# Leaving out sixteen steps of zero products on PE in the opening of a fused attention and gated-MLP kernel

## The chip, the cores and the metric

The kernel runs on one core of one Trainium2 chip. The metric is the device time of one execution in microseconds (us), the median over several executions. Engines are called as in the profile: PE (TensorE), DVE (VectorE), ACT (ScalarE), POOL (GpSimd) and SP (SyncE, whose queue issues the DMAs).

## The reference

Linear attention for 8 batches, 8 heads, 576 tokens and 64 features a head, normalised by the root of its mean square, and then a gated MLP with a product over tokens:

```
kv  = einsum('bhsd,bhse->bhde', k, v)
out = einsum('bhsd,bhde->bhse', q, kv)
x   = out / sqrt(mean(out*out, -1) + 1e-6) * g_norm      # then heads side by side: (8, 576, 512)
h   = gelu(x @ w_in)                                     # tanh form, 512 -> 1024
u, v = h[..., :512], h[..., 512:]
v_n = (v - mean(v)) / sqrt(var(v) + 1e-6) * g_ln
v_s = einsum('ts,bsd->btd', w_sg, v_n) + b_sg[None, :, None]
y   = x + (u * v_s) @ w_out
```

## The kernel before, in words

Every large product is made of three products of float32r halves (high by high, high by low, low by high), so weights and activations are split into a rounded part and a rest: ACT makes the rounded part, DVE or POOL the rest. w_in and w_out come as 64-bit words and are turned into float32 by a chain of integer steps for each of 16 pieces: A (ACT), B, E and L (DVE; L is `word_sign`, line 245), C (POOL, `word_add`, line 248), F (ACT, `weight_high`, line 259) and I (`weight_low`, DVE or POOL, lines 277 to 284). D loads a piece; D16 to D19 load the four blocks of w_sg into two buffers ("stage", line 208), so D18 and D19 can only be issued when the rests of the first two blocks (line 280) are made.

What each engine does, and in which order, is written out by hand in one table, `ORDER`. A name in it is a letter for the step, then the batch, then an index. The steps that matter here, with the tile names that the profile shows:

- k, q: loads of k and v (line 296) and of q (334), issued on SP. SP's queue is in order.
- K (`kv`, line 305, tile pkv): k times v for one block of tokens; c (`kv_high`, line 325) copies the finished matrix out of PSUM on ACT. Batch 0 has K00 to K04, batch 1 K10 to K14.
- o (line 353, tile po): q times that matrix, eight products a batch. f (`o_scale`, line 365 on ACT, 367 on DVE) copies one out with the factor g_norm, e (`o_square`, line 357, ACT, tile sq) squares it, s (`sums`, line 375, tile pss) adds the squares on PE.
- t, j (`rstd`, `newton`, lines 391 to 407): the inverse root by integer estimate and Newton steps, on DVE. For batch 0, T (line 436, y_parts, DVE) and M (line 442, tile pb, PE) spread it over the partitions and x (line 447, DVE) multiplies. From batch 1 on it goes over DRAM (r, lines 413 to 418, tile bc) and x is line 450.
- X, Y (lines 454 and 458): rounded part and rest of x. U (line 540, tile pu) and V (489, pv) are the first products with w_in; P, S and the others follow.
- N (`warm`, line 185, tile warm): two products of a 128x128 block of zeros with 512 columns of zeros. Their PSUM tile is read by nobody.

```
    def warm(*_):
        ps = PS("warm")
        for _ in range(2):
            nc.tensor.matmul(ps, kvh[:, 0, :], kvh.rearrange("p a b -> p (a b)"), start=True, stop=True)
```

The table holds 44 N steps, N00 to N43, all of them ahead of U00, the first product with w_in: 18 from the start to the middle of the run ahead of o00, six more behind them in the same run, and the rest scattered in ones, twos, a three (N33 to N35) and a seven (N37 to N43) between the steps of batch 1 and the first K of batch 2. PE's queue is in order too, so an N step is done before the product behind it, whether that product is ready or not.

Of the kernel before, what the change touches and what calls it, by code (L numbers as in the profile page):

```python
# [10 lines left out]
U32 = mybir.dt.uint32  # L11
# [27 lines left out]

ORDER = """  # L40
    k00 k01 k02 k03 N00 k04 N01 K00 D22 N02 D00 K01 D01 N03 N04 D02 K02 N05 D03 N06 N07 q00 K03 N08 D21 N09 N10 q01
    K04 q02 F22 N11 c00 N12 c01 N13 q03 A00 N14 N15 E00 N16 B00 q10 A01 N17 L00 N18 E01 C00 N19 q11 B01 N20 N21 N22
    D24 F00 N23 L01 k10 I00p o00 F21 o01 k11 f00v e00 o02 e01 f01v C01 o03 A02 f02v k12 s00 e02 B02 o04 F01 E02 o05
    f03a f04v I01p o06 k13 e03 f05v e04 L02 o07 e05 s01 f06a f07v C02 s02 A03 k14 N24 e06 E03 N25 F02 B03 K10 D04
    e07 I02p L03 N26 D05 K11 D06 s03 N27 t00 k20 C03 K12 t01 N28 N29 q12 F03 t02 t03 K13 q13 I03v N30 t04 D16 K14
    t05 N31 j00 c10 j01 N32 c11 D17 j02 A04 o10 j03 j04 o11 e10 B04 k21 N33 A05 E04 N34 j05 e11 N35 B05 f10a T00 s10
    E05 f11a o12 D07 T01 T02 o13 D23 f12a T03 M04 T04 M06 e12 M02 f13v D20 M07 e13 o14 x07v o15 L05 e14 M01 F16 s11
    f14v C05 x01v e15 o16 f15v F17 M00 I16p s12 x06v f16a K20 x00v e16 I17v X00 o17 D18 M05 Y00p x02v M03 D19 f17a
    D08 x05v e17 N36 D09 x03v F20 s13 k22 x04v N37 t10 N38 k23 L04 X01 I21p N39 t11 N40 X02 N41 F18 N42 C04 N43 Y01v
    F19 m0 t12 F04 I19v F05 t13 q20 X03 I05v K21 t14 A06 Y02v Y03p t15 U00 k24 I18v k30 j10 h20 E06 q21 j11 I04v U02  # L50
    u00 j12 n00 A07 j13 n01 j14 U03 E07 u02 j15 B07 r10 n02 L07 K22 u03 n03 U06 C07 h21 k31 B06 c20 c21 r11 F07 U07
    d21 L06 u06 I07v C06 U01 u07 d20 A08 I20v F06 K30 l10 u01 r12 l11 l12 U04 l13 I06v m1 k32 E08 B08 A09 k33 V00
    n10 u04 L08 E09 C08 B09 F08 D10 n11 n12 L09 V01 n13 C09 I08v F09 D11 x10p x11v a00 I09p V02 b00 r13 a01 i20v p00
    i21v q22 y00 q23 K31 b01 z00 o20 k34 w00 p01 o21 e20 V03 k40 e21 a02 y01 b02 x13p z01 h22 w01 U05 p02 i22v a03
    x12p y02 q30 V04 u05 X10 X11 Y10v X12 Y11p b03 z02 K32 Y12v a04 k41 p03 X13 w02 Y13p V10 b04 A10 y03 p04 E10 z03
    V11 B10 L10 y04 C10 w03 z04 D12 F10 w04 S00 A11 I10v E11 S01 a10 g00 b10 G00 B11 H00 p10 S02 L11 J00 C11 g01 y10
    G01 F11 D13 S03 g02 I11p H01 J01 G02 A12 S04 g03 B12 G03 H02 E12 S05 H03 J02 g04 L12 G04 J03 P00 C12 H04 g05 J04
    G05 F12 D14 P01 Q00 I12v A13 S06 E13 Q01 B13 L13 C13 S07 g06 F13 D15 G06 I13v V12 A14 g07 z10 E14 G07 B14 w10
    L14 A15 U15 C14 E15 F14 B15 V13 f20a L15 I14v u15 C15 f21a a11 F15 b11 I15p P03 p11 a12 b12 P02 y11 p12 Q03 z11
    U16 Q02 H05 w11 H06 H07 J05 o22 a13 J06 o23 e22 b13 U12 u16 h23 f22v p13 J07 f23a P06 i23p y13 u12 e23 P07 q31  # L60
# [612 lines left out]
```

## Time and profile before

| | |
|---|---|
| median of 3 runs | 529.02 us (528.95 to 529.67) |
| profiled execution, its own time | 528.13 us |
| its span, first to last instruction | 526.3 us |
| PE busy | 516.1 us, 98% of the span |
| DVE, ACT, POOL busy | 313.5, 200.4, 189.3 us |
| mean granted TensorE clock | 0.996 of full speed |

Busy times are sums over the whole span; a share near 100% says which engine the bulk waits for, and says nothing on the opening, where N steps count as busy too. Times in the rows further down are microseconds from the span's start. In a row of a timeline, the bracket at the end gives the idle time of the engine ahead of the row and who ended it.

### The profile page before, as it was taken

To read this page: it belongs to the slowest core of one execution; us is meant where nothing else is said; L and a number is where in the kernel's file an instruction comes from. 1 tells how busy PE (TensorE), PEld (TensorE's weight loads), DVE (VectorE), ACT (ScalarE), POOL (GpSimd) and SP (SyncE) were. 2 spreads that over 40 slices of the span, in tenths; PEclk is the share of its full clock that TensorE was granted. 3 is DMA by queue.
4 is the path that set the end of the run, shared out by engine and by line. 5 is a ranking of instruction groups with operands and counts; after the bars stand their busy time and mean duration, and the time that the engine had idled before them with its cause. 6 is when DMAs were issued, how large, how long until landed. Compare 5 with 4: busy or idle time off the path is not lost.

```text
span 526.3 us, 10121 instructions
## 1 busy us (share of the span) xinstructions
PE 516.1 (98%) x4032; PEld 476.2 (90%) x4032; DVE 313.5 (60%) x656; ACT 200.4 (38%) x449; POOL 189.3 (36%) x215
## 2 busy tenths in 40 slices
PE   7999899999999999999999999999999999999997
PEld 5765888999999989999999988999999989999997
DVE  0489877867376676645557556646277557841433
ACT  1358545344532336314533325423353325221210
POOL 1345267643345324521044204623117206520230
PEclk9999899999999999999999999999999999999999
DMA  8987684111363455001363144002121221002002
GB/s 249 371 277 263 209 225 152 42 42 52 108 209 94 169 158 149 24 1 45 109 205 102 68 143 100 22 24 68 47 74 45 91 57 40 2 1 91 0 24 69
DMA packets 33723, 55.51 MB, mean 105 GB/s; under 512 B 7308, under 2 KB 9228, under 8 KB 33676
## 3 DMA queue, kind: packets, MB, share of 16 engines
q1 hardware_dynamic: 33676, 54.86, 33.3%
q8 instruction: 32, 0.52, 0.4%
q14 instruction: 15, 0.12, 0.1%
HBM read 44.90 MB, written 9.95 MB: 104 GB/s over the span
## 4 chain that ended last, share of the span: by engine, by line
PE 95%; DMA 2%; POOL 1%; ACT 1%; DVE 0%; SPq 0%; issue 0%; POOLq 0%
PE pu L540 20%; PE pg L554 19%; PE py L586 19%; PE pv L489 18%; PE po L353 5%; PE pkv L305 4%; PE warm L185 4%; PE pg L557 3%; PE pss L375 2%; DMA kv_first<-in_vx 1%; DMA v<-in_vx 1%; POOL xo L458 1%; DVE x L367 0%; SPq L296 0%; ACT sq L357 0%
## 5 line engine op out<-in xcount | busy, mean ns | idle before, releaser
L586 PE MATMUL py<-g,woh 128*128 128x288 f32 x512 | 106.6, 296 | 0.0
L567 POOL TENSOR_TENSOR gt<-gt,u 128x288 f32<-128x288 f32 x64 | 56.4, 887 | 88.4 <-DVE gt L562 79.7
L586 PEld LDWEIGHTS py<-g,woh 128*128 128x128 f32 x512 | 83.7, 188 | 0.3
L554 PE MATMUL pg<-wsh,vh 128*128 128x288 f32 x256 | 75.8, 296 | 0.0
L554 PE MATMUL pg<-wso,vh 128*128 128x288 f32 x256 | 75.6, 295 | 0.0
L586 PE MATMUL py<-g,woo 128*128 128x288 f32 x256 | 75.5, 295 | 0.0
L554 PE MATMUL pg<-wsh,vo 128*128 128x288 f32 x256 | 75.5, 295 | 0.0
L504 POOL TENSOR_SCALAR rs<-mv 128x1 f32<-128x1 f32 x36 | 12.3, 343 | 126.0 <-DVE mv L500 125.3
L574 ACT CAST g<-gt 128x288 fp32r<-128x288 f32 x64 | 27.1, 432 | 79.8 <-POOL gt L567 77.5
L562 DVE SCALAR_TENSOR_TENSOR gt<-pg,glt,b_bc 128x288 f32<-128x288 f32 x64 | 32.8, 515 | 38.2 <-PE pg L557 37.7
L591 DVE SCALAR_TENSOR_TENSOR x<-py,x 128x288 f32<-128x288 f32 x64 | 29.2, 457 | 43.9 <-PE py L586 43.1
L545 ACT ACTIVATE u<-pu 128x288 f32<-128x288 f32 x64 | 26.3, 411 | 62.8 <-PE pu L540 62.3
L586 PEld LDWEIGHTS py<-g,woo 128*128 128x128 f32 x256 | 48.2, 188 | 0.2
L554 PEld LDWEIGHTS pg<-wsh,vh 128*128 128x128 f32 x256 | 48.1, 188 | 0.3
L554 PEld LDWEIGHTS pg<-wso,vh 128*128 128x128 f32 x256 | 48.1, 188 | 0.1
L554 PEld LDWEIGHTS pg<-wsh,vo 128*128 128x128 f32 x256 | 48.2, 188 | 0.0
L540 PE MATMUL pu<-xh,wuh 128*128 128x288 f32 x256 | 45.9, 301 | 0.0
L540 PE MATMUL pu<-xh,wuo 128*128 128x288 f32 x256 | 44.3, 295 | 0.0
L540 PE MATMUL pu<-xo,wuh 128*128 128x288 f32 x256 | 44.3, 295 | 0.0
L499 DVE BATCH_NORM_STATS2 st<-hv 128x6 f32<-128x512 f32 x32 | 22.2, 693 | 33.6 <-ACT hv L494 33.4
L578 DVE TENSOR_TENSOR g<-gt,g 128x288 fp32r<-128x288 f32 x64 | 36.7, 588 | 9.0 <-ACT g L574 9.0
L540 PEld LDWEIGHTS pu<-xh,wuh 128*128 128x128 f32 x256 | 38.1, 190 | 1.6 <-issue 0.5
(108 smaller groups left out, 1025.8 us busy)
## 6 DMA issues: line engine op xcount, KB each, us to landing
q<-in_qT SPq DMA_DIRECT2D x32, 288.0 KB, 4.0
out_y<-x SPq DMA_DIRECT2D x28, 288.0 KB, 2.1
bc<-rd SPq DMA_DIRECT2D x28, 256.0 KB, 4.0
k<-in_kx SPq DMA_DIRECT2D x24, 256.0 KB, 4.4
v<-in_vx SPq DMA_DIRECT2D x24, 256.0 KB, 4.5
kv_first<-in_kx SPq DMA_DIRECT2D x8, 256.0 KB, 5.7
kv_first<-in_vx SPq DMA_DIRECT2D x8, 256.0 KB, 6.1
words<-in_wu SPq DMA_DIRECT2D x4, 512.0 KB, 7.7
```

The source lines that it names most:

```text
L353: nc.tensor.matmul(ps[:, :HS], a, m[:, t], start=(i == 0), stop=(i == len(terms) - 1))
L489: nc.tensor.matmul(pv, a[cc], w[:, cc, :], start=(n == 0), stop=(n == 11))
L499: ve.bn_stats(st, hv_[b, c])
L540: nc.tensor.matmul(pu[:, :HS], w[:, cc, f], a[b, cc][:, t], start=(i == 0), stop=(i == 11))
L545: ac.activation(u_[b, n], part["u", b, n][:, :HS], AF.Gelu_apprx_tanh, scale=W_UP)
L554: nc.tensor.matmul(ps[:, :HS], a[:, d], w[:, c, t], start=(i == 0), stop=False)
L562: ve.scalar_tensor_tensor(g_[b, n], ps[:, :HS], glt[:, dc : dc + 1], b_bc[:, half(n // 4)], op0=ALU.mult, op1=ALU.add)
L567: po.tensor_tensor(g_[b, n], g_[b, n], u_[b, n], op=ALU.mult)
L574: ac.copy(gs_[b, n][0], g_[b, n])
L578: ve.tensor_tensor(lo, g_[b, n], f32(hi), op=ALU.subtract)
L586: nc.tensor.matmul(ps[:, :HS], w[:, dc, block(n % 4)], a, start=(i == 0), stop=(i == 11))
L591: ve.scalar_tensor_tensor(xs, y_[b, n][:, :HS], W_UP, xs, op0=ALU.mult, op1=ALU.add)
```

## The change

Sixteen N steps are taken out of `ORDER`: N18 to N23 ahead of o00, N24 to N32 between the steps of batch 1, and N36 ahead of the last sum of batch 1. The other 28 stay, and all other steps keep their places. One line of the table as an example:

```
-    K04 q02 F22 N11 c00 N12 c01 N13 q03 A00 N14 N15 E00 N16 B00 q10 A01 N17 L00 N18 E01 C00 N19 q11 B01 N20 N21 N22
-    D24 F00 N23 L01 k10 I00p o00 F21 o01 k11 f00v e00 o02 e01 f01v C01 o03 A02 f02v k12 s00 e02 B02 o04 F01 E02 o05
+    K04 q02 F22 N11 c00 N12 c01 N13 q03 A00 N14 N15 E00 N16 B00 q10 A01 N17 L00 E01 C00 q11 B01 D24 F00 L01 k10 I00p
+    o00 F21 o01 k11 f00v e00 o02 e01 f01v C01 o03 A02 f02v k12 s00 e02 B02 o04 F01 E02 o05 f03a f04v I01p o06 k13
```

The table is a line shorter, so each line number below it falls by one in the changed kernel. On PE, from the last K of batch 0 to the last K of batch 1 (pkv is K, warm is N, po is o, pss is s), there stood:

```order
L305 MATMUL pkv<-v,k 64x64 x8
L185 MATMUL warm<-kvh 128x512 x26
L353 MATMUL po<-q,kvf 128x288 x4
L375 MATMUL pss<-sq,ones 32x144 x4
L353 MATMUL po<-q,kvf 128x288 x4
L375 MATMUL pss<-sq,ones 32x144 x8
L185 MATMUL warm<-kvh 128x512 x4
L305 MATMUL pkv<-kv_first 64x64 x8
L185 MATMUL warm<-kvh 128x512 x2
L305 MATMUL pkv<-kv_first 64x64 x8
L375 MATMUL pss<-sq,ones 32x144 x4
L185 MATMUL warm<-kvh 128x512 x2
```

and the same stretch, with what follows up to the three N steps that are left, is now:

```order
L304 MATMUL pkv<-v,k 64x64 x8
L184 MATMUL warm<-kvh 128x512 x14
L352 MATMUL po<-q,kvf 128x288 x4
L374 MATMUL pss<-sq,ones 32x144 x4
L352 MATMUL po<-q,kvf 128x288 x4
L374 MATMUL pss<-sq,ones 32x144 x8
L304 MATMUL pkv<-kv_first 64x64 x16
L374 MATMUL pss<-sq,ones 32x144 x4
L304 MATMUL pkv<-kv_first 64x64 x16
L304 MATMUL pkv<-v,k 64x64 x8
L352 MATMUL po<-q,kvf 128x288 x2
L184 MATMUL warm<-kvh 128x512 x6
```

The run of 26 products ahead of the first po is now 14, and between there and the po of batch 1 no zero product is left. DVE, ACT and POOL keep every instruction in its place. SP keeps the order of its DMAs too, but the two w_sg loads D18 and D19 have changed buffers, and with them their waits. Before, on SP (stage is w_sg, words w_in or w_out; the brackets name the engines and DMA queues waited for):

```order
L211 DMA wl<-in_wsl 128x576 [waits DMAHW6_49,DVE_49]
L208 DMA stage<-in_ws 128x576 [waits DMAHW7_49,DMAHW0_49,Pool_49]
L208 DMA stage<-in_ws 128x576 [waits DMAHW1_49,DVE_49]
L205 DMA words<-in_wo 128x512
L205 DMA words<-in_wo 128x512 [waits DMAHW2_49]
L296 DMA k<-in_kx 128x512 [waits DMAHW3_49,PE_49]
L296 DMA v<-in_vx 128x512 [waits DMAHW4_49]
```

and with the change:

```order
L210 DMA wl<-in_wsl 128x576 [waits DMAHW6_49,DVE_49]
L207 DMA stage<-in_ws 128x576 [waits DMAHW7_49,DMAHW1_49,DVE_49]
L207 DMA stage<-in_ws 128x576 [waits DMAHW0_49,Pool_49]
L204 DMA words<-in_wo 128x512
L204 DMA words<-in_wo 128x512 [waits DMAHW2_49]
L295 DMA k<-in_kx 128x512 [waits DMAHW3_49,PE_49]
L295 DMA v<-in_vx 128x512 [waits DMAHW4_49]
```

The first of the two stage loads now waits for DVE and the second for POOL; it was the other way round.

## Rows read from the trace of the kernel before

**Rows 1.** The page: busy times of PE, and the chain that ended last, by engine

```profile
PE 516.1 (98%) x4032; PEld 476.2 (90%) x4032; DVE 313.5 (60%) x656; ACT 200.4 (38%) x449; POOL 189.3 (36%) x215
...
PE 95%; DMA 2%; POOL 1%; ACT 1%; DVE 0%; SPq 0%; issue 0%; POOLq 0%
```

**Rows 2.** Timeline of PE, 16 to 57 us: start, duration, instruction, idle time before

```profile
16.83 6.19 PE L185 MATMUL warm<-kvh 128*128 128x512 f32 x26
22.86 2.10 PE L353 MATMUL po<-q,kvf 128*128 128x288 f32 x8
...
35.90 0.68 PE L305 MATMUL pkv<-v,k 64*64 64x64 f32 x16
...
55.52 1.12 PE L305 MATMUL pkv<-v,k 128*64 128x64 f32 x16 [0.18 <-DMA v<-in_vx]
56.57 1.26 PE L540 MATMUL pu<-xh,wuh 128*128 128x288 f32 x4
```

**Rows 3.** Timeline of DVE, 20 to 46 us

```profile
22.15 0.14 DVE L269 TENSOR_SCALAR g<-gnt 128x1 f32<-128x1 f32 x1
23.54 0.52 DVE L367 TENSOR_SCALAR x<-po,g 128x288 f32<-128x288 f32 x1 [1.25 <-PE po L353]
...
32.35 0.31 DVE L391 TENSOR_SCALAR rstd<-pss 128x144 f32<-128x144 f32 x1 [1.13 <-PE pss L375]
32.70 1.01 DVE L393 TENSOR_SCALAR rstd<-rstd 128x144 int32<-128x144 int32 x1
...
38.10 0.43 DVE L241 TENSOR_SCALAR w<-w 128x512 int32<-128x512 int32 x1 [0.50 <-ACT w L233]
...
39.64 1.49 DVE L436 SCALAR_TENSOR_TENSOR y_parts<-yh,ext,rstd 32x144 fp32r<-32x144 f32 x4
41.70 0.52 DVE L367 TENSOR_SCALAR x<-po,g 128x288 f32<-128x288 f32 x1 [0.57 <-PE po L353]
...
42.60 0.69 DVE L245 SCALAR_TENSOR_TENSOR w<-words,w 128x512 int32<-128x512 int32 x1
```

**Rows 4.** Timeline of ACT, 28 to 38 us

```profile
30.56 0.41 ACT L357 ACTIVATE sq<-po 128x288 f32<-128x288 f32 x1
33.65 0.62 ACT L259 CAST wuh<-w 128x512 fp32r<-128x512 f32 x1 [2.68 <-POOL w L248]
36.63 0.74 ACT L325 COPY kvf<-pkv 64x256 f32<-64x256 f32 x2 [2.36 <-PE pkv L305]
```

**Rows 5.** Timeline of POOL, 30 to 46 us

```profile
30.74 1.62 POOL L277 TENSOR_TENSOR wuo<-w,wuh 128x512 fp32r<-128x512 f32 x1 [0.73 <-ACT wuh L259]
32.32 1.29 POOL L248 TENSOR_TENSOR w<-w,words 128x512 int32<-128x512 int32 x1
...
44.67 1.44 POOL L280 TENSOR_TENSOR wso<-stage,wsh 128x576 fp32r<-128x576 f32 x1
```

**Rows 6.** Waits of SP's queue, 40 to 62 us: total, times, longest

```profile
SPq L208 <- POOL wso L280: 4.4, 1, 4.4
```

**Rows 7.** The load of v issued at 50.53 us (line 296): time to landing

```profile
DMA to landing us min/median/max: 4.8/4.8/4.8
```

**Rows 8.** Stretches: length, PE busy, PEld, DVE, ACT, POOL, granted clock, DMA share, GB/s

```profile
22.90:28.80 5.90, 5.44 (x42) 3.13 (x40) 4.48 (x9) 4.27 (x11) 3.09 (x4) 1.00 1.04 336
...
37.50:48.20 10.70, 10.70 (x98) 6.93 (x97) 9.47 (x23) 8.38 (x19) 4.49 (x3) 1.00 0.78 275
...
51.60:54.20 2.60, 0.01 (x1) 0.02 (x1) 2.32 (x4) 2.09 (x6) 0.80 (x1) 1.00 0.96 336
54.20:57.60 3.40, 3.20 (x36) 2.94 (x37) 3.40 (x7) 1.34 (x2) 1.41 (x1) 0.50 0.58 188
```

**Rows 9.** Timeline of POOL, 81 to 91 us

```profile
81.28 1.30 POOL L450 TENSOR_TENSOR x<-x,bc 128x512 f32<-128x512 f32 x1 [2.03 <-DMA bc<-rd]
...
84.34 1.28 POOL L450 TENSOR_TENSOR x<-x,bc 128x512 f32<-128x512 f32 x1
86.74 1.43 POOL L458 TENSOR_TENSOR xo<-x,xh 128x576 fp32r<-128x576 f32 x1 [1.12 <-ACT xh L454]
```

More of the change, by code (lines that the diff above doesn't have):

```diff
@@ L46 @@
[L46 to L60, printed above, removed]
@@ new lines @@
+    o00 F21 o01 k11 f00v e00 o02 e01 f01v C01 o03 A02 f02v k12 s00 e02 B02 o04 F01 E02 o05 f03a f04v I01p o06 k13
+    e03 f05v e04 L02 o07 e05 s01 f06a f07v C02 s02 A03 k14 e06 E03 F02 B03 K10 D04 e07 I02p L03 D05 K11 D06 s03 t00
+    k20 C03 K12 t01 q12 F03 t02 t03 K13 q13 I03v t04 D16 K14 t05 j00 c10 j01 c11 D17 j02 A04 o10 j03 j04 o11 e10 B04
+    k21 N33 A05 E04 N34 j05 e11 N35 B05 f10a T00 s10 E05 f11a o12 D07 T01 T02 o13 D23 f12a T03 M04 T04 M06 e12 M02
+    f13v D20 M07 e13 o14 x07v o15 L05 e14 M01 F16 s11 f14v C05 x01v e15 o16 f15v F17 M00 I16p s12 x06v f16a K20 x00v
@@ new lines @@
+    e16 I17v X00 o17 D18 M05 Y00p x02v M03 D19 f17a D08 x05v e17 D09 x03v F20 s13 k22 x04v N37 t10 N38 k23 L04 X01
+    I21p N39 t11 N40 X02 N41 F18 N42 C04 N43 Y01v F19 m0 t12 F04 I19v F05 t13 q20 X03 I05v K21 t14 A06 Y02v Y03p t15
+    U00 k24 I18v k30 j10 h20 E06 q21 j11 I04v U02 u00 j12 n00 A07 j13 n01 j14 U03 E07 u02 j15 B07 r10 n02 L07 K22
+    u03 n03 U06 C07 h21 k31 B06 c20 c21 r11 F07 U07 d21 L06 u06 I07v C06 U01 u07 d20 A08 I20v F06 K30 l10 u01 r12
+    l11 l12 U04 l13 I06v m1 k32 E08 B08 A09 k33 V00 n10 u04 L08 E09 C08 B09 F08 D10 n11 n12 L09 V01 n13 C09 I08v F09
@@ new lines @@
+    D11 x10p x11v a00 I09p V02 b00 r13 a01 i20v p00 i21v q22 y00 q23 K31 b01 z00 o20 k34 w00 p01 o21 e20 V03 k40 e21
+    a02 y01 b02 x13p z01 h22 w01 U05 p02 i22v a03 x12p y02 q30 V04 u05 X10 X11 Y10v X12 Y11p b03 z02 K32 Y12v a04
+    k41 p03 X13 w02 Y13p V10 b04 A10 y03 p04 E10 z03 V11 B10 L10 y04 C10 w03 z04 D12 F10 w04 S00 A11 I10v E11 S01
+    a10 g00 b10 G00 B11 H00 p10 S02 L11 J00 C11 g01 y10 G01 F11 D13 S03 g02 I11p H01 J01 G02 A12 S04 g03 B12 G03 H02
+    E12 S05 H03 J02 g04 L12 G04 J03 P00 C12 H04 g05 J04 G05 F12 D14 P01 Q00 I12v A13 S06 E13 Q01 B13 L13 C13 S07 g06
@@ new lines @@
+    F13 D15 G06 I13v V12 A14 g07 z10 E14 G07 B14 w10 L14 A15 U15 C14 E15 F14 B15 V13 f20a L15 I14v u15 C15 f21a a11
+    F15 b11 I15p P03 p11 a12 b12 P02 y11 p12 Q03 z11 U16 Q02 H05 w11 H06 H07 J05 o22 a13 J06 o23 e22 b13 U12 u16 h23
+    f22v p13 J07 f23a P06 i23p y13 u12 e23 P07 q31 Q06 y12 O06 z12 P05 Q07 z13 w12 O07 w13 P04 Q05 O05 o24 Q04 o25
+    e24 O04 U14 e25 h30 f24a i30p U13 u14 f25a q32 o26 u13 o27 f26v e26 U11 h31 c30 i31p c31 d30 U17 u11 d31 f27a
+    q33 e27 o30 u17 o31 f30v s20 h32 f31a i32p K40 t20 e30 t21 e31 o32 k42 o33 t22 e32 f32v U10 k43 h33 f33v q40 e33
@@ new lines @@
+    i33p t23 o34 u10 o35 e34 S10 q41 e35 t24 t25 j20 j21 j22 S11 g10 j23 G10 j24 h40 K41 j25 H10 i40p g11 J10 S12
+    k44 G11 k50 r20 H11 S13 g12 q42 J11 G12 S14 H12 g13 J12 G13 S15 H13 g14 r21 J13 G14 r22 P11 H14 g15 J14 G15 P12
+    Q11 l20 l21 l22 l23 S16 m2 Q12 n20 n21 n22 S17 n23 g16 x21p x20v P10 G16 g17 X20 r23 G17 X21 Y20v P13 Y21p Q10
+    K42 Q13 H15 H16 J15 k51 H17 J16 J17 P17 P16 Q17 O17 x23v x22p P15 Q16 O16 X22 P14 Q15 f34a Y22v O15 f35a X23 o36
+    Q14 o37 Y23p e36 f36v O14 V20 h41 f37v c40 i41p c41 d40 e37 d41 q43 s30 a20 b20 K50 t30 p20 U26 k52 t31 t32 y20
@@ new lines @@
+    k53 t33 z20 V21 t34 u26 w20 t35 j30 j31 j32 j33 V22 a21 j34 j35 b21 r30 p21 V23 y21 a22 z21 b22 r31 w21 p22 r32
+    K51 a23 y22 U23 b23 z22 k54 k60 w22 p23 U21 l30 u23 l31 l32 l33 y23 m3 U22 z23 n30 n31 n32 x30p u21 w23 o40 u22
+    o41 e40 x31p U25 h42 f40v e41 n33 f41a V24 r33 i42v u25 q50 o42 a24 o43 f42a K52 b24 h43 U20 k61 f43v p24 e42
+    e43 i43p y24 o44 u20 o45 e44 U24 x33p e45 q51 x32v h50 z24 U27 i50v u24 w24 S20 q52 u27 X30 X31 Y30v S21 X32 g20
+    X33 Y31v G20 S22 g21 Y32p H20 J20 S23 Y33p g22 G22 V30 g23 G21 G23 H21 H22 J21 H23 J22 S24 a30 J23 b30 p30 P21
@@ new lines @@
+    g24 G24 y30 P23 H24 Q21 J24 P20 Q23 S25 Q20 V31 g25 G25 P22 a31 b31 S26 Q22 H25 p31 J25 y31 S27 g26 G26 H26 V32
+    g27 z30 J26 G27 z31 w30 H27 J27 P27 w31 a32 b32 U35 Q27 p32 O27 y32 P26 z32 u35 w32 f44a U36 Q26 f45a O26 U32
+    u36 o46 u32 P24 f46v e46 U31 Q24 O24 P25 u31 o47 Q25 U33 h51 f47v O25 c50 i51v c51 U37 e47 d50 q53 u33 d51 o50
+    u37 o51 f50a s40 f51v h52 K60 t40 e50 i52v e51 o52 t41 q60 o53 t42 k62 f52a t43 V33 t44 f53a k63 t45 h53 j40 j41
+    e52 i53p j42 e53 o54 a33 o55 q61 j43 U34 e54 b33 h60 j44 p33 e55 j45 U30 r40 u34 i60p y33 K61 u30 z33 k64 w33
@@ new lines @@
+    r51 a41 b41 V42 r52 p41 k74 y41 z41 V43 a42 l50 l51 l52 l53 w41 m5 b42 U40 n50 p42 a43 n51 n52 n53 x50p b43 V44
+    u40 x51v p43 y42 r53 z42 y43 w42 z43 K72 a44 w43 U45 b44 U42 p44 u45 y44 z44 o60 o61 x53p U44 f60a w44 h62 x52p
+    u42 S40 u44 i62v X50 X51 S41 Y50p X52 Y51v q70 e60 e61 f61a S42 Y52p X53 g40 g41 S43 g42 Y53p G42 V50 G40 G41
+    H40 J40 H41 g43 V51 H42 J41 a50 G43 J42 H43 b50 o62 J43 a51 p50 P41 f62v e62 b51 P43 y50 p51 Q41 y51 P40 Q43 P42
+    Q40 o63 Q42 o64 f63a S44 h63 e63 i63v e64 S45 q71 g44 G44 H44 o65 g45 S46 e65 J44 G45 h70 i70p H45 S47 J45 q72
@@ new lines @@
+    X60 J53 r63 X61 Y60p H54 P51 g55 J54 Y61p P52 g56 Q51 n61 G56 n62 P53 G55 Q52 n63 S57 x63v x62p Q53 P50 X62 g57
+    G57 X63 Y62p Y63v V60 H55 H56 Q50 H57 J55 J56 J57 P55 a60 b60 P54 Q55 p60 O55 y60 P56 z60 Q54 O54 w60 f74a P57
+    Q56 f75a O56 o76 Q57 o77 e76 f76v O57 U66 f77a e77 s70 u66 U61 t70 t71 t72 t73 t74 U65 t75 u61 j70 j71 j72 U63
+    j73 u65 j74 j75 r70 V61 u63 r71 V62 a61 r72 b61 p61 V63 y61 a62 l70 z61 l71 l72 l73 w61 m7 b62 U60 a63 n70 p62
+    n71 n72 n73 x70p b63 V64 u60 y62 x71p z62 w62 U67 p63 r73 a64 b64 U62 y63 u67 p64 z63 y64 U64 u62 w63 z64 u64
@@ new lines @@
+    w64 S60 X70 x72p X71 x73v S61 X72 Y70v Y71p X73 S62 g60 g61 G60 G61 H60 S63 g62 Y72p H61 Y73v V70 G62 J60 H62
+    J61 J62 V71 g63 a70 G63 b70 H63 p70 J63 P61 y70 a71 b71 P63 Q61 p71 y71 P62 Q63 P60 Q62 S64 Q60 S65 g64 G64 H64
+    S66 g65 J64 G65 S67 H65 g66 J65 G66 U76 H66 g67 z70 J66 G67 z71 w70 U75 u76 H67 w71 J67 P65 u75 P66 Q65 O65 P67
+    Q66 O66 U77 Q67 O67 P64 u77 U72 Q64 O64 V72 u72 V73 a72 b72 p72 U70 y72 a73 z72 b73 U71 w72 u70 p73 U74 y73 u71
+    z73 w73 S70 u74 S71 g70 G70 H70 S72 g71 J70 G71 U73 H71 g72 J71 G72 S73 u73 H72 J72 S74 g73 G73 H73 S75 g74 J73
@@ L106 @@
+    G74 P71 H74 g75 J74 G75 P73 Q71 H75 O71 J75 S76 Q73 O73 S77 g76 G76 H76 P70 g77 J76 G77 P72 Q70 H77 O70 J77 P74
+    Q72 O72 P75 Q74 O74 P76 Q75 O75 P77 Q76 O76 Q77 O77
 """.split()
```

57 lines of the change are left out of this document (10 added, 47 removed).

## The prediction, made before the changed kernel had run

> **What bounds the kernel now.** I read the page first: PE is busy for 516.1 of 526.3 us, and the chain that ended last is 95% PE [rows 1]. So the bulk is PE's own work, and a change ahead of it can only matter by the moment at which that bulk starts. The timeline of PE has it at 56.57 us: the first product with w_in, behind two K steps that waited for v [rows 2]. From there on the list of PE's waits is empty, to the end. So the question is how much earlier the product at 56.57 starts, and whether what feeds PE later keeps up. In the opening PE looks busy throughout, but 18 us of that are zero products; there I read the waits of the other engines: DVE waits for PE at 23.54, 32.35 and 41.70 [rows 3], ACT at 36.63 [rows 4], and SP's queue waits 4.4 us for POOL [rows 6]. These name the path.
>
> **The change part by part.**
>
> *A zero product's price.* The 26 products ahead of o00 lie between 16.83 and 22.86 [rows 2]: 0.232 us each, 0.464 a step. Sixteen steps are 7.4 us of PE. That is the ceiling, and the path takes little of it.
>
> *Six steps ahead of o00: 1.2 us of their 2.8.* PE would reach o00 at 20.1 instead of 22.86, if its q is there (no row of mine shows the landing; even if it came at 21.5, the copy named next would not be later, since the first product takes some 0.7). What waits for o00 is the DVE copy at 23.54, after 1.25 idle. The instruction ahead of it ends at 22.29 [rows 3]. So the copy starts at about 22.3: **1.2 earlier**. The other 1.6 becomes idle time on PE.
>
> *N24 to N26 and the sum: 2.1.* Copies and squares of batch 0 follow one another on DVE and ACT and end with the square at 30.56 to 30.97 [rows 4]; being fed by that copy, it moves 1.2, to an end at 29.75. The sum behind it ends in time for DVE's 32.35 [rows 3], but was then held not by the square but by PE's queue, zero products included. Three of these steps (1.4) are gone on top of the 1.2, so PE is there 2.6 earlier and waits for the square: the sum, 0.45 long, ends at about 30.2, and DVE starts at 30.3, **2.1 earlier**.
>
> *The root on DVE: 1.5 at its end.* DVE now meets POOL's two instructions at 30.74 and 32.32 [rows 5], which have only moved by 1.2, in other places. The row at 32.70 took 1.01 us and ended just after POOL's row of 32.32; I let one DVE row wait for that POOL row again. ACT's row at 33.65 waits for the same POOL row, and DVE's 34.30 for ACT, so at this point the gain is only 1.0. A second wait, 0.50 for ACT at 38.10 [rows 3], goes: ACT stood behind the copies at 36.63, which waited 2.36 for PE [rows 4], and PE's K14 at 35.90 [rows 2] has seven more steps (3.2 us) out of its way. That makes 1.5: the four rows from 39.64 end at 39.6 instead of 41.13.
>
> *N30 to N32 and the wait at 41.70: 2.1.* DVE then idled 0.57 for PE [rows 3]. With the copies of 36.63 at about 33.3, behind ACT's 33.65 less 1.0 [rows 4], the products of 37.54 [rows 2] run near 34.2; the three N steps that stay (1.4) and four more products end near 38.3. So DVE goes on at 39.6: **2.1 earlier**, and with it the L245 at 42.60 [rows 3] and POOL's L280 of 44.67 [rows 5], which ends SP's wait of 4.4 [rows 6].
>
> *SP and the loads of batch 2: 2.1.* Behind that wait SP issues two stage loads, two words, and the k and v for which PE waits at 55.52. The swapped waits of the two stage loads price at nothing: both were issued one behind the other and both rests are needed before the second. Were the first to be late by the 0.6 between the two rests, its ACT copy stands behind other work. The last v took 4.8 us to land [rows 7], as before, so the K behind it starts at 53.4 instead of 55.52, and the products of 56.57 at about **54.5, 2.1 earlier**. N36's two products (0.46) sit ahead of a sum that waits for its square; I give them nothing, and 0.5 in the range.
>
> *The clock: 0 to 1.05 given back.* PE was idle from 51.6 to 54.2, the granted clock then stood at 0.50 (the lower level, 1.2 GHz) until 57.6, and at 1.00 (2.4 GHz) in all the stretches ahead, also where PE had short waits, 5.44 busy in 5.90 [rows 8]. Today 1.05 of dense work falls into the low stretch (56.57 to 57.6), which costs 0.5. If that stretch moves with the idle time, this is unchanged. If it stays where it is, 3.1 of dense work falls into it, costing 1.55, or 1.05 more. I take 0.4, between the two. New idle on PE is shorter than the 2.6 that was followed by the fall: about 1.3 near 22 to 23.4, 1.0 near 29, 1.7 from 32.5 to 34.2. By the rows I price these at no fall. The Trainium skill ("TensorE: Matmul & The Clock Gate", section "A second HAM failure mode: psum-queue depth-cycling") tells of a kernel whose PE idled shortly but often between groups of products, and whose clock went to and fro for it; no row here shows that, and by it the sum would be that of the first rival.
>
> *Later: the gain must pass 81 to 91 us.* The chain of waits leaves PE once more, for POOL's xo rows at 86.74 and 89.79, which PE awaits at 91.2. They begin with ACT work that PE itself feeds, but POOL's x of 81.28 waits for a DMA, and the x of 84.34 ends at 85.62 [rows 9]. If that DMA does not move, the row at 86.74 can come 1.1 earlier and no more. It should move, since its issue goes back over DVE and POOL rows to a K of batch 2 near 62, which PE reaches earlier. Bounds 1.1 and 2.1.
>
> **Sum.** 2.1 less 0.4 is 1.7 us. The profiled execution took 528.13 (526.3 of span, 1.8 around it) and would take 526.4. It lies 0.9 under the median of the three runs; against that median the forecast is 529.02 - 1.7 = **527.3 us**.
>
> **The rivals.**
>
> *Slower: the clock falls in the opening.* With its filling gone PE does 5.3 us of real products between 22.9 and 28.8, and 3 between 28.8 and 37.5. If the clock falls there, it can be low for the products with q and for K20, in the stretch 37.5 to 48.2, where PE is busy all the time and DVE and ACT wait for it by turns [rows 8]. A low stretch as long as the one seen (3.4) costs at most 1.7 where PE is waited for. One such stretch eats the gain: 529.0. Two turn it: 527.3 + 3.4 = 530.7; low from 28.8 to 48, with 8 us of real products in the last part at half speed less the waits they fill, gives some 533. It decides from two stretches on PE's path. For it: no stretch with so much short idling exists in the trace. Against it: the full clock with 5.44 busy in 5.90, and that slower products fill the gaps by themselves.
>
> *No change: lost on the way.* The path above passes from engine to engine six times. If POOL and DVE meet badly (rows like the 1.01 at 32.70 instead of a few tenths), or if the chain at 81 to 91 holds its DMA, 0.6 to 1.2 is left: 527.9 to 528.4.
>
> *More than forecast.* If the low stretch is missed altogether and SP's issues close up, PE's bulk may start up to 3.1 earlier: 525.9.
>
> **How the numbers follow.** No change can be told from one here within 0.2%, 1.06 us: 527.96 to 530.08. The forecast (525.9 to 527.9) has 0.55, the lost gain and one low stretch, both within the bound, 0.28, and two or more low stretches 0.17. So faster 0.55, same 0.28, slower 0.17. The range goes from 525.8, the largest gain, to 530.6, where about a tenth is left above; the forecast's own range is 525.9 to 527.9.
>
> **What would show it.** Right: PE's first po near 20.3; the DVE copy near 22.3; DVE's L391 (now L390) near 30.3; its y_parts ending near 39.6; SP's two stage loads near 44; PE's first pu near 54.5; a granted clock of 1.00 from 16 to 50 us; and no PE wait longer than now behind 91 us. Wrong: a clock of 0.50 anywhere from 23 to 48 us, a square or copy that keeps its old time, or a first pu that is earlier while POOL's xo at 89.79 is not.

## The result: slower by 0.8%, and the profile after

The changed kernel took 532.92 us (median of 7 runs, 531.76 to 534.45), the kernel before 529.43 in the same session (7 runs, 528.42 to 530.07): ratio 1.0077, 95% interval 1.0056 to 1.0098. Forecast were 527.3 us and a range up to 530.6; it went the other way. The profiled execution took 531.76 us with a span of 530.0, 3.7 more than the span of 526.3 before. In two of the kernels further down (the changed kernel again, and the same padded) a single run of 1262 and of 1268 us is counted in the median and left out of the ratio.

The page of the changed kernel, busy times and the chain that ended last (to set beside [rows 1]):

```profile
PE 510.1 (96%) x4000; PEld 471.5 (89%) x4000; DVE 316.1 (60%) x656; ACT 200.8 (38%) x449; POOL 189.1 (36%) x215
...
PE 89%; DMA 8%; POOL 1%; SPq 1%; ACT 1%; issue 0%; DVE 0%; DVEq 0%; POOLq 0%
```

PE has 32 products less and is busy 6.0 us less, and yet the whole is longer: what was PE's share of the chain is now DMA's, 8% where there were 2%. PE's timeline from the first product with q on (po; to set beside [rows 2]) says where:

```profile
22.04 2.18 PE L352 MATMUL po<-q,kvf 128*128 128x288 f32 x8 [1.05 <-POOL w L247]
...
29.77 0.69 PE L304 MATMUL pkv<-kv_first 128*64 128x64 f32 x16 [0.76 <-DMA kv_first<-in_vx]
...
33.26 0.69 PE L304 MATMUL pkv<-kv_first 128*64 128x64 f32 x16 [1.47 <-DMA kv_first<-in_vx]
34.83 0.68 PE L304 MATMUL pkv<-v,k 64*64 64x64 f32 x16 [0.88 <-DMA v<-in_vl]
36.45 2.07 PE L352 MATMUL po<-q,kvf 128*128 128x288 f32 x4 [0.94 <-ACT kvf L324]
37.90 2.77 PE L184 MATMUL warm<-kvh 128*128 128x512 f32 x6
...
56.13 0.69 PE L304 MATMUL pkv<-v,k 128*64 128x64 f32 x16 [3.99 <-DMA v<-in_vx]
57.45 1.12 PE L304 MATMUL pkv<-v,k 128*64 128x64 f32 x16 [0.63 <-DMA v<-in_vx]
58.50 1.33 PE L539 MATMUL pu<-xh,wuh 128*128 128x288 f32 x4
```

Four short waits stand where the zero products stood. Behind them four products with q took 2.07 us and six zero products 2.77; before it was

```profile
37.54 1.18 PE L353 MATMUL po<-q,kvf 128*128 128x288 f32 x4
38.35 1.77 PE L185 MATMUL warm<-kvh 128*128 128x512 f32 x6
```

The rows at 56.13 and 57.45 are K21, the second K of batch 2, in two parts (K20 runs near 46 us, and the seven N steps from N37 on stand between the two). The wait ahead of it grew from 2.60 to 3.99, and the first product with w_in (pu), 56.57 before, stands at 58.50. The stretches of the changed kernel (columns as in rows 8) give the clock:

```profile
28.80:37.50 8.70, 4.53 (x83) 3.43 (x80) 7.86 (x18) 3.00 (x7) 3.57 (x3) 0.95 1.06 332
36.60:40.10 3.50, 3.50 (x9) 2.55 (x10) 3.01 (x11) 2.56 (x6) 0.00 (x0) 0.51 1.05 385
...
57.10:60.50 3.40, 3.05 (x24) 2.97 (x25) 3.37 (x12) 0.67 (x1) 0.00 (x0) 0.50 0.47 128
```

and the first of them before:

```profile
28.80:37.50 8.70, 8.70 (x110) 5.82 (x107) 7.26 (x17) 2.90 (x8) 4.08 (x3) 1.00 0.82 248
```

There are two stretches at the lower level (0.50, 1.2 GHz; called low stretches from here on): the one behind the wait for K21's v, as in before [rows 8], and a new one from 36.6 to 40.1 us. PE had been busy for 4.53 of the 8.70 us from 28.8, where before it had been busy throughout. DVE's timeline (to set beside [rows 3]) shows an early gain and its loss:

```profile
23.07 0.52 DVE L366 TENSOR_SCALAR x<-po,g 128x288 f32<-128x288 f32 x1
...
31.03 0.31 DVE L390 TENSOR_SCALAR rstd<-pss 128x144 f32<-128x144 f32 x1 [0.28 <-PE pss L374]
...
38.94 1.50 DVE L435 SCALAR_TENSOR_TENSOR y_parts<-yh,ext,rstd 32x144 fp32r<-32x144 f32 x4
42.26 0.52 DVE L366 TENSOR_SCALAR x<-po,g 128x288 f32<-128x288 f32 x1 [1.82 <-PE po L352]
```

0.47 earlier at the first copy, 1.32 at the root's first row, 0.70 at y_parts. Then DVE waits 1.82 us for products that start late and run at the lower clock, and the copy that stood at 41.70 stands at 42.26, 0.56 late. From PE's po at 36.45 to this copy it is 5.81 us; before, from 37.54 to 41.70, it was 4.16, so the lower clock cost some 1.65 here. The two stage loads whose waits were swapped are issued at 47.29 instead of 46.13, but closer together, and the last v behind them at 51.09 instead of 50.53: late by the same 0.56, so the swap added nothing. The flight of that v, 6.2 us instead of 4.8, makes the rest of the 1.93 by which the first pu is late. By PE's first product with w_out (105.5 us before, 108.2 now) 2.7 of the 3.7 us of loss stand; most of the rest is one wait of 0.7 us for a DVE copy further on.

One more row does not fit a story of the clock alone. The eighth load of the program (v of K03) is issued at 4.0 us in both kernels, when nothing that differs between them has run. Time from its issue to its landing, before:

```profile
DMA to landing us min/median/max: 6.1/6.1/6.1
```

and in the changed kernel:

```profile
DMA to landing us min/median/max: 9.7/9.7/9.7
```

SP's queue passes this on. It waits for these loads before it issues the weights, and the first q, issued at 10.77 us before, is issued at 13.98. (The bracket of the po at 22.04 names POOL, but this q landed at 21.90.) The chain that ended last, followed back from PE's K14, is then a row of loads, each issued when the one before it has landed (start, duration):

```profile
13.98 7.92 DMA q<-in_qT
22.29 5.90 DMA kv_first<-in_vx
28.21 6.58 DMA v<-in_vl
34.83 0.71 PE pkv L304 x16
```

In the kernel before PE's own work, zero products included, stands in that place of the chain from 7.62 to 23.5 us and from 27.49 to 50.3 us.

### The profile page after: what moved, and what is told of

It is laid out like the page before. It is cut to its first block, busy times and chain, and to the rows that moved or that the text cites. A ratio compares the mean times of both kernels' runs of the same rounds, so it can differ in the third digit from the quotient of the medians.

```text
span 530.0 us, 10057 instructions
## 1 busy us (share of the span) xinstructions
PE 510.1 (96%) x4000; PEld 471.5 (89%) x4000; DVE 316.1 (60%) x656; ACT 200.8 (38%) x449; POOL 189.1 (36%) x215
## 4 chain that ended last, share of the span: by engine, by line
PE 89%; DMA 8%; POOL 1%; SPq 1%; ACT 1%; issue 0%; DVE 0%; DVEq 0%; POOLq 0%
PE pu L539 19%; PE pg L553 19%; PE py L585 19%; PE pv L488 18%; PE po L352 5%; PE pkv L304 3%; PE pg L556 3%; DMA kv_first<-in_vx 3%; PE pss L374 2%; DMA q<-in_qT 1%; DMA v<-in_vl 1%; DMA v<-in_vx 1%; DMA out_y<-x 1%; PE warm L184 1%; SPq L295 1%; POOL xo L457 1%
```

## The experiments

All ratios are to the kernel before, run on the same chip in the same session; the number of runs is in brackets. There were four sessions, each on another chip: the first four experiments, the next four, the next three and the last four. Kernels of different sessions are best compared by their ratios. "Behind N43" is the place behind the last fourteen zero products ahead of K21, where PE waits for v. Some of the texts on record call this step K20.

### Which half of the change, and the wait ahead of K21

**Six steps out** (N18 to N23 alone):

```diff
-A01 N17 L00 N18 E01 C00 N19 q11 B01 N20 N21 N22 D24 F00 N23 L01
+A01 N17 L00 E01 C00 q11 B01 D24 F00 L01
```

> Only the six steps ahead of the first product with q are out; the ten later ones stay. Clock theory (without its filling PE has short idle times, the granted clock falls to 0.50 between 28 and 50 us in most executions, and slow products on the path cost more than the steps): here nearly all of the filling is still there, so the clock stays at 1.00 up to 50 us and the kernel is 0 to 1.2 us faster than before (the first copy on DVE comes 1.2 earlier): 528.2 to 529.4. Load theory (the changed kernel is slow because its first loads of k and v landed some 3 us later than before, which has nothing to do with the N steps): the time follows the landings of the first loads in this run's trace, 529 if they are as before. Path theory (the sum of the prediction, which needs no clock): 1.0 to 1.2 faster.

Measured: 530.69 us (12 runs), ratio 1.0031 (1.0009 to 1.0053). Slower, against the clock and the path expectations: the clock held up to 55 us, and the eighth load took 9.4 us, as the load expectation would have it.

**Ten steps out** (N24 to N32 and N36 alone):

```diff
-k14 N24 e06 E03 N25 F02
+k14 e06 E03 F02
...
-x05v e17 N36 D09
+x05v e17 D09
```

> Only the ten later steps (N24 to N32 and N36) are out; the six ahead of the first product with q stay. Clock theory: the clock falls in the stretch 28 to 50 us as in the changed kernel, mean granted clock 0.99 or lower, 531.5 to 533.5. Load theory: as before, 529, unless its first loads are late. Path theory: 0 to 1 faster, 528.4 to 529.4.

Measured: 533.62 us (7 runs), ratio 1.0076 (1.0044 to 1.0108). The trace has a low stretch from 36.3 to 43.1 us; its eighth load took 9.4 us too.

**The changed kernel again**, with no edit:

> The changed kernel once more, for a second trace and more clocks. Clock theory: 532 to 534 again, with at least two low stretches of the clock ahead of 57 us, also when the first loads land as in the kernel before. Load theory: when the first loads land as in the kernel before (the fourth load by 7.5 us) the time is 529 or less.

Measured: 533.02 us (12 runs), ratio 1.0065 (1.0041 to 1.009). Its five runs with a mean clock of 0.983 to 0.987 took 533.6 to 535.1 us, the six with 0.990 to 0.994 530.3 to 532.5; the runs of before beside them had 0.993 to 0.999. The profiled execution, 530.67 us, has no low stretch ahead of 53 us, against the clock expectation; its eighth load was late again (8.8 us).

**A bridge** (before, with six more zero steps, N50 to N55, behind N43):

```diff
-C04 N43 Y01v
+C04 N43 N50 N51 N52 N53 N54 N55 Y01v
```

> The kernel before with six more N steps behind N43, in the 2.6 us in which PE idles for v ahead of the second K of batch 2. Clock theory: the clock no longer falls at 54.2, the K and the first products with w_in run at 1.00, and 0.5 to 1.0 us are gained: 528.4 to 528.9. If zero products don't hold the clock, or if the low stretch costs nothing: 529.4, or up to 0.3 more where the six steps (2.8 us) reach past the arrival of v.

Measured: 526.85 us (11 runs), ratio 0.9945 (0.9926 to 0.9964): more work on PE makes the kernel 2.5 us faster. PE's timeline, with the twelve products in the place of the 2.60 us of idle time:

```profile
47.94 6.23 PE L185 MATMUL warm<-kvh 128*128 128x512 f32 x26
54.10 0.69 PE L305 MATMUL pkv<-v,k 128*64 128x64 f32 x16
55.23 0.69 PE L305 MATMUL pkv<-v,k 128*64 128x64 f32 x16 [0.44 <-DMA v<-in_vx]
55.84 0.80 PE L540 MATMUL pu<-xh,wuh 128*128 128x288 f32 x4
```

K21 runs at 0.69 a part where it took 1.12, the first products with w_in take 0.80 where they took 1.26 [rows 2]. The trace has no low stretch between 13 and 520 us. So PE's idle time ahead of K21 brings the low stretch of the kernel before. Between the two traces the span differs by 1.2 us only (526.3 and 525.1), with a low stretch of 3.4 us in before; a second trace of before (below) has one of 6.8. The runs bear out the rest: of all 114 runs of before in the four sessions, the ten with a mean clock of 0.998 or more took 526.4 to 528.2 us, as with the bridge, and the 49 with 0.994 or less had a median of 530.1. So the low stretch was worth most of the 2.5 us. And each part of the change alone loses, the ten steps more than the six by their medians (the intervals overlap a little).

### The length of PE's program

The late loads were in all kernels with fewer products on PE than before has, and not in the others. The chip does not part the two: on the first one the bridge's eighth load took 6.5 us beside 8.8 to 9.4 of the three shorter programs, on the second one it is 9.0 of the one shorter program beside 5.8 to 7.4. To tell chance from cause, the next kernels get their count back by short products of 64 columns behind PE's last product, where PE has nothing left to do.

**The changed kernel, padded** with 32 of them:

```diff
+    def pad(*_):
+        ps = PS("pad")
+        for _ in range(2):
+            nc.tensor.matmul(ps[:, :64], kvh[:, 0, :], kvh[:, 0, :64], start=True, stop=True)
...
-O77
+O77 W00 W01 W02 W03 W04 W05 W06 W07 W08 W09 W10 W11 W12 W13 W14 W15
```

> The changed kernel with 32 short zero products (64 columns) behind its last product, where PE idles while the last stores land, so that PE's program has as many instructions as before. Clock theory: nothing changes, 532 to 534, mean clock 0.983 to 0.994. Program theory (the first loads land late, the eighth near 14 us instead of 10.8, in the four kernels with a shorter PE program, because the program's size shifts where things lie in memory): the eighth load lands near 11 us and 1 to 1.5 us are gained, 531 to 532.

Measured: 531.58 us (10 runs), ratio 1.0043 (1.0011 to 1.0074). The eighth load took 7.2 us, as the program theory had it; a low stretch from 34.3 to 37.8 us stays.

**Before again**, one execution:

> The kernel before, unchanged, for a second trace. Program theory: the eighth load lands near 11 us again. If the first loads merely vary between executions, it can land anywhere between 10.8 and 14. Clock theory: clock 1.00 from 13 to 50 us whatever the loads do, and one or two low stretches near 54 us.

Measured: 527.94 us. Its eighth load took 5.8 us.

**The changed kernel with the bridge:**

> The changed kernel with the six N steps behind N43. It is to part the low stretch at 54 us from those in the opening. Clock theory: the first is gone, those between 28 and 50 us stay, so it is 2 to 3 us faster than the changed kernel but 2 to 4 slower than the kernel before with the same six steps (526.85): 529 to 531. If the changed kernel's loss is all at 54 us, it comes to 527.

Measured: 532.49 us (12 runs), ratio 1.0067 (1.0041 to 1.0093). The bridge alone does not help the changed kernel, and both expectations missed. Its eighth load took 9.0 us, and the trace has low stretches from 33.6 to 40.4 and from 57.4 to 64.3 us. Its five runs with a mean clock of 0.995 to 0.999 still took 530.1 to 533.3 us, so the clock is not the whole loss.

**Six steps moved** (N18 to N23 out, the bridge in, so PE's count is that of before):

> The six steps ahead of the first product with q are moved behind N43; the other 38 stay, and the number of instructions is that of the kernel before. Clock theory: no low stretch, 526 to 527, as fast as with the six steps added, or up to 1.2 faster by the earlier first copy. Program theory: the eighth load lands near 11 us; then the 1.4 us that the kernel without the six was slower than before are explained, and it is 525.7 to 526.9. If the six steps are needed where they stand, 528 or more.

Measured: 526.23 us (12 runs), ratio 0.9935 (0.9911 to 0.9959), within the first two expectations.

**Six steps out, padded** (twelve short products at the end):

> Only N18 to N23 out, as in the run of that name without a bridge, and twelve short zero products (64 columns) behind PE's last product, which bring PE's instruction count back to that of before. Length theory: loads that were issued before anything differed came late in the kernels with a shorter PE program (the eighth load landed at 13.97 us there, at 10.76 and 10.88 in before), so with the count restored the eighth load lands by 12 us, the last v of K20 needs about 5 us instead of 7.0, the first product with pu starts a us earlier than in before and the time is 528 to 529.5. Clock theory alone: the loads are late by chance, PE waits as long ahead of the v loads, and the time stays at 530.7 with the low clock at 55 to 62 us.

Measured: 528.17 us (12 runs), ratio 0.997 (0.995 to 0.9991); without the pad it was 1.0031 (1.0009 to 1.0053). Twelve products that run after all other products make the kernel 0.0061 of its time faster, 3.2 us. The clock alone does not explain it: at the same mean clock of 0.994 the six runs without the pad took 530.3 to 533.7 us and the five with it 528.4 to 529.0, while before had medians of 529.7 and 529.8 at this clock in the two sessions. The last v still took 6.3 us, not the five expected.

**All out, bridge and pad** (twenty short products):

> The changed kernel with six zero steps behind N43 and twenty short zero products behind PE's last product, so that PE's count is that of before. Length theory: the eighth load lands by 12 us, K13 and K14 wait little, no or one low stretch in the opening, and the time is 527 to 529 (before the bridge alone: 532.5). Clock theory: the opening still has a low stretch at 34 to 43 us, since the ten later steps are missing, and the time is 529.5 to 532. If the length says nothing: 532.5 again, eighth load at 13 to 14 us.

Measured: 529.45 us (12 runs), ratio 1.0009 (0.9992 to 1.0027); without the pad 1.0067 (1.0041 to 1.0093). The eighth load landed at 12.1 us; the time lies between the two theories' ranges, and the opening has its low stretch.

**Before, padded** (twelve):

> The kernel before with twelve short zero products behind PE's last product: the price of the pad itself and a control of the length theory on the long side. Both theories: the eighth load at 10.5 to 12 us, the clock as in before, and the time 529.2 plus 0 to 1.0 for the pad.

Measured: 529.14 us (12 runs), ratio 1.0003 (0.999 to 1.0017): the pad itself costs and gives nothing that shows.

The profiled executions side by side. "Eighth load" and "last v of K21" are times from issue to landing, the wait is the one ahead of K21's first part, and "first pu" is when the first product with w_in starts:

| kernel | products on PE | eighth load | last v of K21 | wait ahead of K21 | first pu |
|---|---|---|---|---|---|
| before | 4032 | 6.1 | 4.8 | 2.60 | 56.57 |
| six out, padded | 4032 | 6.4 | 6.3 | 3.41 | 56.05 |
| six moved | 4032 | 7.4 | 5.3 | none | 54.99 |
| all out, bridge, pad | 4032 | 8.1 | 5.4 | 0.57 | 57.90 |
| all out, padded | 4032 | 7.2 | 5.5 | 3.22 | 55.27 |
| six out | 4020 | 9.4 | 7.0 | 4.39 | 58.30 |
| ten out | 4012 | 9.4 | 7.0 | 4.94 | 61.31 |
| all out, bridge | 4012 | 9.0 | 7.1 | 2.38 | 59.98 |
| changed kernel | 4000 | 9.7 | 6.2 | 3.99 | 58.50 |
| changed kernel again | 4000 | 8.8 | 5.9 | 3.52 | 56.72 |

With 4032 products or more (twelve traces in all) the eighth load took 5.8 to 8.1 us; with fewer (five traces) 8.8 to 9.7. Two pairs of kernels that differ in the pad alone have intervals that do not meet; in the third, the changed kernel and its padded form, they overlap. The two kernels of each pair ran on different chips, so these comparisons go by way of before.

### What the ten later steps are for

With the count restored and the bridge in, all sixteen out still take 529.45 us, six moved 526.23. PE's timeline of the former:

```profile
28.48 0.69 PE L310 MATMUL pkv<-kv_first 128*64 128x64 f32 x16 [0.77 <-DMA kv_first<-in_vx]
...
32.68 0.69 PE L310 MATMUL pkv<-kv_first 128*64 128x64 f32 x16 [2.01 <-DMA kv_first<-in_vx]
34.39 1.12 PE L310 MATMUL pkv<-v,k 64*64 64x64 f32 x16 [1.02 <-DMA v<-in_vl]
36.45 2.26 PE L358 MATMUL po<-q,kvf 128*128 128x288 f32 x4 [0.94 <-ACT kvf L330]
38.09 3.09 PE L184 MATMUL warm<-kvh 128*128 128x512 f32 x6
```

and two of its stretches:

```profile
28.80:37.50 8.70, 4.29 (x71) 3.31 (x67) 6.31 (x16) 2.14 (x5) 2.75 (x2) 0.81 1.06 305
34.10:40.90 6.80, 5.58 (x26) 4.10 (x26) 4.32 (x14) 3.55 (x8) 0.00 (x0) 0.50 1.05 387
```

The eighth load is earlier here than in any shorter program (8.1 us, though the most of the twelve), and PE waits for loads all the same once nothing covers the wait; then it has 6.8 us at the lower level, in which four products with q take 2.26 us and six zero products 3.09 (1.18 and 1.77 in before). DVE's copy behind them:

```profile
42.77 0.52 DVE L372 TENSOR_SCALAR x<-po,g 128x288 f32<-128x288 f32 x1 [2.15 <-PE po L358]
```

With six steps moved the same two rows read

```profile
36.26 1.18 PE L353 MATMUL po<-q,kvf 128*128 128x288 f32 x4
40.42 0.52 DVE L367 TENSOR_SCALAR x<-po,g 128x288 f32<-128x288 f32 x1 [0.56 <-PE po L353]
```

(35.80 and 39.97 in its repeat). From that po to the copy it is 4.16 to 4.17 us there and 6.32 here. So the waits themselves put the po off by 0.2 to 0.65 us, and the lower clock behind them costs 2.15, of the 2.7 to 2.9 by which the first pu is later (57.90 beside 54.99 and 55.22).

Is that a cost of all ten steps, or of having none of them? Four kernels, based on the one with six steps moved and padded to its count:

**N24 to N26 out:**

> The kernel with N18 to N23 moved behind N43 (526.23 us), without N24, N25 and N26, and with six short zero products behind PE's last product, so that PE's count is that of before. Path theory (the sum of the prediction: 0.464 us a step up to the copy and the root of batch 0): 1.0 to 1.4 us come off where no load is waited for, and the time is 525 to 525.5. Clock theory (these steps hold the clock where PE waits for the loads of K10 to K14): a low stretch at 33 to 43 us, and 527 to 529.

Measured: 525.73 us (12 runs), ratio 0.9948 (0.993 to 0.9965).

**N30 to N32 out:**

> The kernel with N18 to N23 moved behind N43, without N30, N31 and N32, and with six short zero products behind PE's last product. Path theory: these six products stand ahead of the copy that ends the root's wait at 41.70 us in before, 1.0 to 1.4 us come off, 525 to 525.5 us. Clock theory: PE waits for kvf there instead, a low stretch at 36 to 43 us, 527 to 529.

Measured: 525.22 us (6 runs), ratio 0.9934 (0.9914 to 0.9953).

**One product instead of two in each of the ten:**

```diff
-        for _ in range(2):
+        for _ in range(1 if 10 * m + n in (24, 25, 26, 27, 28, 29, 30, 31, 32, 36) else 2):
```

> The kernel with N18 to N23 moved behind N43, with one zero product instead of two in each of the ten later steps (N24 to N32 and N36), and ten short zero products behind PE's last product. Path theory: half of the gain of ten steps, 1 to 2 us, 524.5 to 525.5 us. Clock theory: half of the cover is left; if the clock holds with it, 525 to 526.5; if a low stretch comes at 34 to 43 us, 527 to 528.5, about half way to the 529.45 of the kernel with all ten out, the bridge and the count restored.

Measured: 525.28 us (10 runs), ratio 0.9948 (0.9923 to 0.9974).

**Six moved, again:**

> The kernel with N18 to N23 moved behind N43 once more, on the chip of the other three, as their reference: ratio to before 0.9935 again (0.991 to 0.996), clock 0.999 to 1.0, no low stretch ahead of 520 us.

Measured: 526.75 us (12 runs), ratio 0.9965 (0.9948 to 0.9982).

No trace of the four has a low stretch between 13 and 520 us. The medians of the three lie 1.0 to 1.5 us below that of their reference, as if a part of the ten steps were a cost on the path, but their ratios (0.9934, 0.9948 and 0.9948) hardly leave the range of the two measurements of six moved (0.9935 and 0.9965): a gain is not shown, only that a part can go without a loss. What loses is taking all ten. And half of each step is not safe in every execution: two of its ten runs have a mean clock of 0.996 and took 528.9 and 529.2 us, the other eight 0.997 to 1.0 and 524.4 to 525.8. With N30 to N32 out PE's opening reads

```profile
32.87 0.68 PE L311 MATMUL pkv<-v,k 64*64 64x64 f32 x16
34.48 1.21 PE L359 MATMUL po<-q,kvf 128*128 128x288 f32 x4 [0.94 <-ACT kvf L331]
35.31 1.74 PE L185 MATMUL warm<-kvh 128*128 128x512 f32 x6
```

with the same wait of 0.94 for kvf as above, and no fall behind it; and the stretch that held 4.29 and 4.53 of PE's work holds

```profile
28.80:37.50 8.70, 7.76 (x98) 5.41 (x98) 7.24 (x22) 4.08 (x9) 2.47 (x2) 1.00 1.03 337
```

This kernel, 525.22 us, beats the kernel before and the changed one, at a span of 523.5; that it beats six moved alone is not shown.

## Why the prediction was wrong, by its own steps

**Three steps failed.** The first is "By the rows I price these at no fall" in the step on the clock. The rows it went by had one idle time of 2.60 ahead of the fall and a single 0.46 with none; several waits in a row were not among them. They came (0.76, 1.47, 0.88 and 0.94), and the clock fell at 36.6 us. The passage of the Trainium skill that the prediction set aside ("TensorE: Matmul & The Clock Gate", section "A second HAM failure mode: psum-queue depth-cycling") tells of short but frequent idling between groups of products. The traces agree that short waits can do it, though here they are waits for loads: no single wait ahead of the fall was longer than 2.01 us in the kernel with bridge and pad, and 1.47 in the changed kernel.

The second is "The last v took 4.8 us to land [rows 7], as before" in the step on SP and the loads of batch 2. In the changed kernel it took 6.2 us, in its repeat 5.9. It belongs to something that neither the sum nor a rival had: loads land later in a kernel whose PE program is shorter, the eighth load among them, which is issued before anything differs. This put the first q off too, and with it PE's first po (22.04, not 20.1; with six steps moved, where loads are early, it stands at 20.03 and the copy at 22.27, as forecast).

The third is the assumption that a zero product taken out leaves the next real one free. "PE's K14 at 35.90 [rows 2] has seven more steps (3.2 us) out of its way" put the kvf copies near 33.3 and the products behind them near 34.2. In the profiled execution ACT's row stands at 35.56 and the po at 36.45, since K13 and K14 waited for their loads. How far the step fails depends on when the loads land in an execution: in the changed kernel's repeat the po stands at 34.80, with the copy that was forecast for 39.6 at 39.71, in the padded form at 34.23, but with bridge and pad at 36.45 again. The prediction had no row for these loads, because in before the zero products covered them; it should have bounded them.

In the profiled execution the first pu misses its forecast by 4.0 us (58.50 for 54.5): 1.4 is the flight of the last v, and 2.66 the copy at 42.26 instead of 39.6, of which some 1.65 is the lower clock and the other 1.0 late loads. The repeat kept the clock in the opening and still had its first pu at 56.72, with the last v and a q of batch 1 late and a low stretch of 6.8 us (53.6 to 60.4) across it.

**The pieces, in the ratios of the runs.** Six steps out with the count kept: 0.997, or 1.6 us gained (1.2 forecast on the way). All sixteen out with the count kept: 1.0043, so the ten cost 0.0073, 3.9 us, where 0.9 more was forecast to come off. The missing count: from 1.0043 to 1.0065 or 1.0077, 1.2 to 1.8 us, the least certain of the three by its overlapping intervals. The sum, -1.6 + 3.9 + 1.2 to 1.8, is 3.5 to 4.1 us, which is what the two measurements of the change give (1.0065 and 1.0077); as a difference of the same ratios it must close, so it is a division of the loss and no proof of it. With the bridge in, the ten cost as much (0.9935 to 1.0009, 3.9 us).

**Right:** the price of a zero product, 0.232 at the higher clock; the path by DVE's copy, the root and SP; the copy at 22.3 where loads are early (22.27 with six moved). The first pu near 54.5 was not met with all sixteen out; the nearest is 55.27 in the padded form. Six moved has 54.99, and 53.39 with N30 to N32 out too, but these two have the bridge, which the sum did not, so that they are no test of it. "Later: the gain must pass 81 to 91 us" was a fair caution: in the profiled execution of six moved, the slowest of its runs, PE waits 1.7 us for POOL's second xo, which stands at 89.72 as if nothing had been gained (89.79 before). It is a matter of the execution, for in the repeat that row stands at 87.97, without a wait, and with N30 to N32 out at 86.22.

**Too small:** the low stretch behind K21, which "costs 0.5". That counts only the products with w_in. Between the traces of before and of the bridge the first four of these products differ by 0.46 us, and K21's second part adds 0.44, which the step left out. Other executions of before had a longer stretch (6.8 us in the second trace), and by the runs it was worth most of 2.5 us.

**The rival with the right sign,** the clock falling in the opening, had the mechanism and a chance of 0.17. It decided "from two stretches on PE's path"; the profiled execution shows one in the opening and the old one behind K21, as in before, and the rest came from the loads. The changed kernel's trace had one of 3.5 us in the opening, its repeat none, and the clock means of the runs, 0.983 to 0.994, say that it differs from run to run.

## What to carry to other kernels

Fill that looks like waste on a busy engine can be the cover of waits that the profile cannot show while it stands: bound those waits by the issue and the flight of the loads before pricing the fill as path. Take such fill out in parts and keep some of it in each gap: with the bridge in and the count kept, parts of the ten steps could go without a loss, and all of them could not. And ask of a wait on PE ahead of dense work what the clock is behind it; twelve products put into that wait gained 2.5 us, and twelve taken out ahead of o00 gained 1.6 with the count kept.

## What the runs showed of the hardware that was not expected

- The clock fell to 0.50 behind a row of waits of which the longest was 1.47 us (changed kernel, 36.6 us) and 2.01 us (all out, bridge, pad, 34.1 us); it stayed at 1.00 behind a single 0.94 in the same place (N30 to N32 out).
- Loads that were issued at 4.0 us, before any difference had run, took 8.8 to 9.7 us in five kernels' traces with fewer than 4032 products on PE and 5.8 to 8.1 in twelve with as many or more, and 12 or 20 short products behind everything else took 0.0061 and 0.0058 off the ratio to before, 3.1 to 3.2 us. Why, no run shows: it may be the length or anything in the program's placement that goes with it. It was not tried to shorten the program at its end alone, nor another engine's.
- In two executions of the kernel before, the opening differed by 2 us (the first pu at 56.57 and 54.61) and the spans by 0.1 (526.3 and 526.2): the earlier one waited 3.13 instead of 2.60 for v and had 6.8 us at the lower level instead of 3.4, and by the first product of pv (70.2 and 70.3) its lead was gone.
